# Two attention and token-MLP layers on one core: the order of SyncE's final waits

## The chip, the core and the metric

The kernel runs on one core of one Trainium2 chip. Five engines work side by side in that core, each through an instruction stream of its own: TensorE (PE), VectorE (DVE), ScalarE (ACT), GpSimd (POOL) and SyncE (SP). They are ordered among each other by semaphores alone. SyncE does no arithmetic here: it issues all the transfers (DMAs) and waits on semaphores. The metric is the device time of one execution in microseconds (us); lower is better.

## The reference, cut to what matters

```
x = A_x                                            # 1 x 2048 x 512, bf16
x = x + A(layernorm(x)); x = x + B(layernorm(x))   # layer 1
x = x + A(layernorm(x)); x = x + B(layernorm(x))   # layer 2, same weights
A: 32 heads of width 16, each query sees the 256 positions up to its own;
   softmax, times V, times wo (512 x 512)
B: h = layernorm(x); u = gelu(h^T . w1 (2048 x 1792) + b1); y = u . w2 (1792 x 2048) + b2; x + y^T
```

A mixes positions inside a window, B mixes all positions for each of the 512 columns. The result, 2048 x 512 in bf16, is 2 MB.

## The kernel before

The 2048 positions stand as 16 blocks of 128 on the partitions; x stays in on-chip memory (`x_sb`) through both layers and is written to the output (`out_dram`) only in the last stage. Attention goes through the sequence in chunks of 4 or 8 windows of 64 queries: scores on TensorE (L705), the exponential on ScalarE (L720), masks on GpSimd (L741), the product with V on TensorE (L758), then a transpose and a division. Between those, TensorE takes projection, wo and MLP matmuls (all of them through the helper at L526) as filler. The MLP's first product ends in L908, its gelu in L923. Its second product, y, is made a block of 128 positions at a time: fourteen matmuls add up into one bank of the accumulator, VectorE adds bias and residual (`resy`, L949) and SyncE stores the block (L997). The last block, `y_last`, is cut into pieces of 256, 128 and 128 columns, each with its own addition (L935) and its own store (L938). So the output leaves in 15 stores of 128 rows x 512 columns and 3 smaller ones.

Every operation is recorded in a `Graph`, and a list stored with the kernel (`ORDER`) fixes in which order each engine takes them. `Graph.emit` then writes the five streams. It gives every transfer one of 24 semaphores (`NDMA`), in turn: transfer number n, in SyncE's order, raises semaphore n modulo 24, and `rr` is the count of transfers at the end. A semaphore's transfer may only be issued when the one 24 before it has landed. `dcnt[k]` is the value that semaphore k has when all its transfers have landed.

When SyncE has issued its last transfer it waits, in the last lines of `emit`, until each of the 24 semaphores has its full count (L252). Then it leaves the block by a branch (L339) and meets the other four engines at a barrier, which ends the program. The barrier is run by GpSimd: it waits until all have signalled and then releases them.

The waits of those last lines are not written into the program in the order in which the loop names them. [...] In the program as built, that list is for the kernel before, from the first to the last:

```
12 | 13, 11 | 14, 10 | 15, 9 | 16, 8 | 17, 7 | 18, 6 | 19, 5 | 20, 4 | 21, 3 | 22, 2 | 23, 1 | branch: 0
```

That is: the names 0 to 23 of the loop come out from the middle of the list to its two ends. The last transfer of this kernel, the store of the last 128 columns, raises semaphore 13; the one before it, a store of a whole block, raises 12.

Of the kernel before, what the change touches and what calls it, by code (L numbers as in the profile page):

```python
# [93 lines left out]
class Graph:  # L94
# [104 lines left out]
    def emit(self, block):  # L199
        mark = {}  # L200
        cnt = {e: 0 for e in self.ENGS}
        dcnt = [0] * self.NDMA
        dlast = [None] * self.NDMA
        rr = 0
        for e in self.ENGS:
            for o in self.order[e]:
                if o.dma:
                    k = rr % self.NDMA
                    rr += 1
                    if dlast[k] is not None:  # L210
                        o.extra.append(dlast[k])
                    dlast[k] = o
                    dcnt[k] += 16 * o.parts
                    mark[o.idx] = (("d", k), dcnt[k])
                else:
                    cnt[e] += 1
                    mark[o.idx] = (e, cnt[e])

        know = {e: {} for e in self.ENGS}
        at_issue = {}  # L220
        waits = {}
        for o in sorted(self.ops, key=lambda o: o.pos):
            e = o.eng
            need = [d for d in {x.idx: x for x in o.deps + o.extra}.values() if not (e == "tensor" and d.eng == "tensor")]
            kn = know[e]
            best = {}
            for d in sorted(need, key=lambda d: -d.pos):
                s, v = mark[d.idx]
                if kn.get(s, 0) >= v:
                    continue  # L230
                best[s] = v
                kn[s] = v
                for s2, v2 in at_issue[d.idx].items():
                    if kn.get(s2, 0) < v2:
                        kn[s2] = v2
            waits[o.idx] = list(best.items())
            at_issue[o.idx] = dict(kn)
        sem = lambda s: self.dsem[s[1]] if isinstance(s, tuple) else self.sem[s]
        decs = {"sync": block.sync, "tensor": block.tensor, "vector": block.vector, "scalar": block.scalar,
                "gpsimd": block.gpsimd}  # L240
        for e in self.ENGS:
            def body(eng, e=e):
                for o in self.order[e]:
                    for s, v in waits[o.idx]:
                        eng.wait_ge(sem(s), v)
                    ins = o.fn(eng, o.cols32) if o.flex else o.fn(eng)
                    for i in ins if o.parts > 1 and o.dma else [ins]:
                        i.then_inc(sem(mark[o.idx][0]), 16 if o.dma else 1)
                if e == "sync":
                    for k in range(self.NDMA):  # L250
                        if dcnt[k]:
                            eng.wait_ge(self.dsem[k], dcnt[k])  # L252
            decs[e](body)
# [777 lines left out]
```

## Time and profile before

| what | us |
|---|---|
| median of 3 runs | 434.5 (434.42 to 434.79) |
| the profiled execution, its own time | 434.05 |
| its span, from the first instruction to the last | 432.3 |
| last TensorE matmul begins | 428.9 |
| last VectorE instruction ends | 429.5 |
| last store issued by SyncE, from and to | 429.64, 430.07 |
| last store landed | 431.19 |
| SyncE's branch out of the block | 431.90 |

The profile names an engine's instructions by the line of the kernel that made them. "L252 SPq" is SyncE's own queue at line 252: the semaphore-only instructions of the final waits. The start that a row gives for a waiting instruction is the moment at which its waits were over, as the rows of the end show: each begins right behind what it waited for. Semaphore and branch instructions aren't counted as busy time of an engine, so the page's first table, in which PE has 98% of the span, does not contain them; they are found by asking for their line, or by asking who waited for whom. The trace gives instructions and landings in nanoseconds, and the times with two or three decimals in this text are from it.

### The profile page before, as it was taken

The page shows a single profiled execution, that of the slowest core. Times are in us where ns is not written, and L with a number is a line of the kernel's source. Part 1 is how long each engine was busy: PE and PEld are TensorE (multiplying, and loading weights), DVE is VectorE, ACT ScalarE, POOL GpSimd, SP SyncE. Part 2 cuts the span into 40 slices and gives each one's busy share as a digit, 9 for nine tenths or more (in the row PEclk, how much of TensorE's full clock was granted, in tenths as well). Part 3 has the DMA queues.
Part 4 walks back from the last instruction along what each step waited for, and adds up shares of the span by engine and source line. Part 5 has one row for each costly group of instructions (what it writes and reads, how often), then busy time and mean ns, then how long its engine had stood idle before and what let it go on. Part 6 is the DMA issues. An engine that isn't in the chain of part 4 may idle for free.

```text
span 432.3 us, 14319 instructions
## 1 busy us (share of the span) xinstructions
PE 422.5 (98%) x6192; PEld 189.1 (44%) x6192; DVE 302.6 (70%) x566; ACT 324.0 (75%) x375; POOL 240.0 (56%) x359
## 2 busy tenths in 40 slices
PE   8898999999999999999999999999999999999997
PEld 7444444443434444443444444443443444444453
DVE  7999988997789868637565868788876377512133
ACT  4999999999998965509989999999999961330000
POOL 5698959697796651002677588778794741000000
PEclk9999999999999999999999999999999999999999
DMA  8735613540322556435352340330221455772453
GB/s 250 205 63 91 150 41 71 100 106 15 83 46 52 137 144 174 136 73 155 72 153 59 101 111 2 80 50 3 55 64 38 123 150 151 201 217 65 125 155 109
DMA packets 95023, 45.12 MB, mean 104 GB/s; under 512 B 27888, under 2 KB 94960, under 8 KB 94960
## 3 DMA queue, kind: packets, MB, share of 16 engines
q1 hardware_dynamic: 94960, 44.20, 39.9%
q8 instruction: 49, 0.80, 0.8%
q14 instruction: 14, 0.11, 0.1%
HBM read 33.56 MB, written 2.10 MB: 82 GB/s over the span
## 4 chain that ended last, share of the span: by engine, by line
PE 87%; ACT 8%; DVE 3%; POOL 1%; DMA 0%; issue 0%
PE PS L526 60%; PE PS L705 10%; PE PS L758 8%; PE PS L908 8%; ACT pt L720 7%; POOL pt L741 1%; DVE xh_sb L499 1%; DVE rl L796 1%; DMA x_sb<-in_A_x_dram 0%; DVE stats L475 0%; ACT kbd L596 0%; ACT vst L645 0%; DVE x_sb L949 0%; DVE vst L643 0%; DVE qT L586 0%
## 5 line engine op out<-in xcount | busy, mean ns | idle before, releaser
L720 ACT ACTIVATE pt<-PS 128x1024 bf16<-128x1024 f32 (+1 forms) x304 | 282.7, 1032 | 9.5 <-PE PS L705 7.6
L741 POOL TENSOR_TENSOR pt<-pt,ldm 128x256 int32<-128x256 int32 (+2 forms) x266 | 176.4, 690 | 55.7 <-ACT pt L720 52.1
L526 PE MATMUL PS<-xh_sb,w1b 128*128 128x512 bf16 x292 | 72.6, 381 | 0.1
L526 PE MATMUL PS<-uT,w2b 128*128 128x512 bf16 (+2 forms) x308 | 68.2, 360 | 0.0
L526 PE MATMUL PS<-xhT,wqkv 128*128 128x512 bf16 (+1 forms) x288 | 66.7, 357 | 0.8 <-DVE rl L796 0.4
L705 PE MATMUL PS<-qT,kbd 32*128 32x64 bf16 (+4 forms) x1552 | 60.2, 247 | 2.6 <-ACT pt L720 1.3
L949 DVE SCALAR_TENSOR_TENSOR x_sb<-PS,b2col,x_sb 128x512 bf16<-128x512 f32 x31 | 22.8, 748 | 55.6 <-PE PS L526 55.5
L492 POOL TENSOR_TENSOR rstd<-agg,mhalf 128x2 f32<-128x2 f32 (+1 forms) x34 | 23.4, 691 | 56.8 <-DVE agg L478 56.6
L705 PEld LDWEIGHTS PS<-qT,kbd 32*128 32x128 bf16 x1552 | 22.7, 92 | 61.1 <-ACT pt L720 44.0
L796 DVE STREAM_TRANSPOSE rl<-PS 128x1024 f32<-128x1024 f32 x31 | 38.5, 1242 | 14.0 <-PE PS L758 13.7
L758 PE MATMUL PS<-pt,vb 64*17 64x128 bf16 (+4 forms) x3104 | 44.0, 248 | 1.2 <-ACT pt L720 0.9
L526 PEld LDWEIGHTS PS<-uT,w2b 128*128 128x128 bf16 x308 | 27.6, 98 | 31.9 <-issue 3.2
L475 DVE BATCH_NORM_STATS2 stats<-x_sb 128x6 f32<-128x512 bf16 x62 | 40.9, 675 | 0.9 <-DMA x_sb<-in_A_x_dram 0.5
L526 PE MATMUL PS<-uT,pt 128*128 128x512 bf16 x168 | 40.8, 379 | 0.0
L758 PEld LDWEIGHTS PS<-pt,vb 64*17 64x17 bf16 x3104 | 31.6, 84 | 17.9 <-ACT pt L720 6.2
L526 PEld LDWEIGHTS PS<-xh_sb,w1b 128*128 128x128 bf16 x292 | 24.7, 97 | 32.8 <-issue 5.4
L526 PEld LDWEIGHTS PS<-xhT,wqkv 128*128 128x128 bf16 x288 | 24.3, 97 | 28.4 <-issue 5.3
L526 PE MATMUL PS<-wqkv,xhT 128*128 128x512 bf16 x128 | 34.4, 381 | 0.6 <-ACT pt L720 0.5
L908 PE MATMUL PS<-xh_sb,w1b 128*128 128x512 bf16 x156 | 34.6, 379 | 0.0
L923 ACT ACTIVATE uT<-rl,b1col 128x512 bf16<-128x512 f32 x28 | 18.1, 711 | 21.5 <-DVE rl L919 21.3
L526 PE MATMUL PS<-wo_sb,oT 128*128 128x512 bf16 x128 | 33.4, 381 | 0.0
L499 DVE TENSOR_SCALAR xh_sb<-x_sb,agg,rstd 128x512 bf16<-128x512 bf16 x64 | 28.8, 473 | 2.6 <-POOL rstd L492 2.5
(70 smaller groups left out, 331.6 us busy)
## 6 DMA issues: line engine op xcount, KB each, us to landing
w1b<-in_B_w_dram SPq DMA_DIRECT2D x109, 128.0 KB, 2.7
w2b<-in_B_w_dram SPq DMA_DIRECT2D x70, 128.0 KB, 2.7
pt<-in_B_w_dram SPq DMA_DIRECT2D x42, 128.0 KB, 3.2
vb<-vst SPq DMA_DIRECT2D x64, 68.0 KB, 2.1
out_dram<-x_sb SPq DMA_DIRECT2D x15, 128.0 KB, 1.9
x_sb<-in_A_x_dram SPq DMA_DIRECT2D x3, 512.0 KB, 6.7
wqkv<-in_A_wqkv_dram SPq DMA_DIRECT2D x4, 256.0 KB, 4.4
wqkv<-in_A_wqkv_dram SPq DMA_DIRECT2D x1, 512.0 KB, 5.8
```

Of the source, the lines that this page charges most:

```text
L475: op("vector:stat", lambda e: e.bn_stats(st[:, 0:6], bank(ft) if ft else x_sb[:, t, :]), reads=[ft or f"x{t}"], writes=[("st", i)], cost=d ...
L492: op("gpsimd:rstd", lambda e: e.tensor_tensor(rstd[:, t0:t1, 0], agg[:, t0:t1, 1], mhalf[:, 0:1].to_broadcast([P, t1 - t0]), op=ALU.pow), ...
L499: op("vector:xh", lambda e: e.tensor_scalar(xh_sb[:, t, :], x_sb[:, t, :], agg[:, t, 0:1], rstd[:, t, :], op0=ALU.subtract, op1=ALU.mult), ...
L526: return e.matmul(o, lhsT=w, rhs=x, start=start, stop=stop, skip_group_check=True)
L705: last = e.matmul(bank(tt[r // 2], r % 2)[:, base + c0 * 64:base + (c0 + n) * 64], lhsT=kbd[32 * r:32 * r + 32, tk[0][o].slot, jj].rearran ...
L720: op("scalar:exp", lambda e, ts=ts, tp=tp, i=i, cols=cols: e.activation(probs(tp)[:, i, 0:cols, :], pair(ts)[:, :, 0:cols].rearrange("p r ...
L741: return e.tensor_tensor(v, v, m, op=ALU.mult)
L758: last = e.matmul(bank(t, h)[32 * r:32 * r + 17, i + q0 * 64:i + (q0 + n) * 64], lhsT=vb[64 * h:64 * h + 64, tk[1].slot, jj, 4 * o + r, :] ...
L796: op("vector:od", lambda e, t=tod, tr=tr: e.transpose(rl[:, tr.slot:tr.slot + 2].rearrange("p a b -> p (a b)"), pair(t)), reads=[(tod, i) ...
L908: last = e.matmul(bank(tu, tt), lhsT=v()[:, sc - b0, k0 + tt * P:k0 + (tt + 1) * P], rhs=xh_sb[:, sc, :], start=(sc == b0), stop=(sc == NT ...
L923: op("scalar:gelu", lambda e, ft=ft, tt=tt: e.activation(uT[:, ft, :], rl[:, tmps[tt].slot], ACTF.Gelu_apprx_tanh, bias=b1col[:, ft:ft + 1 ...
L949: op("vector:resy", lambda e: e.scalar_tensor_tensor(x_sb[:, t, :], bank(ft), b2col[:, t:t + 1], x_sb[:, t, :], op0=ALU.add, op1=ALU.add), ...
```

## The change

The loop over the 24 semaphores at the end of `emit` no longer names them from 0 to 23, but in a list that starts from the last transfer:

```
--- before.py
+++ after.py
@@ -247,7 +247,8 @@
                     for i in ins if o.parts > 1 and o.dma else [ins]:
                         i.then_inc(sem(mark[o.idx][0]), 16 if o.dma else 1)
                 if e == "sync":
-                    for k in range(self.NDMA):
+                    late = [(rr - 1 - j) % self.NDMA for j in range(self.NDMA)]
+                    for k in late[:1] + late[1::2] + late[2::2][::-1]:
                         if dcnt[k]:
                             eng.wait_ge(self.dsem[k], dcnt[k])
             decs[e](body)
```

`late` is 13, 12, 11, ... down to 0, then 23, ... down to 14: the semaphores from the last transfer's backwards. The loop names 13 first, then 12, 10, 8 and so on, and the odd places from the far end last. After the same spreading from the middle to the two ends, the list in the program as built is

```
14 | 15, 16 | 17, 18 | 19, 20 | 21, 22 | 23, 0 | 1, 2 | 3, 4 | 5, 6 | 7, 8 | 9, 10 | 11, 12 | branch: 13
```

It is the order in which the last 24 transfers were issued. There are twelve semaphore-only instructions and a branch as before, and the streams of the five engines are otherwise the same, row by row. All lines behind the edit have a number that is higher by one (L997 becomes L998).

More of the change, by code (lines that the diff above doesn't have):

```diff
@@ L249, in body @@
                 if e == "sync":
-                    for k in range(self.NDMA):
+                    late = [(rr - 1 - j) % self.NDMA for j in range(self.NDMA)]
+                    for k in late[:1] + late[1::2] + late[2::2][::-1]:
                         if dcnt[k]:
```

## The prediction

> **What bounds the kernel now.** I read the page's totals and the chain first, to see what the span is made of; then the last 12 us of SyncE's queue in order of time, who waited for whom there, and last the final waits and the branch by their lines.
>
> ```profile
> span 432.3 us, 14319 instructions
> PE 422.5 (98%) x6192; PEld 189.1 (44%) x6192; DVE 302.6 (70%) x566; ACT 324.0 (75%) x375; POOL 240.0 (56%) x359
> PE 87%; ACT 8%; DVE 3%; POOL 1%; DMA 0%; issue 0%
> ```
>
> TensorE bounds 98% of the span. The edit touches none of its instructions, so nothing can be won there; all that the change can move lies behind the last matmul (begun at 428.9). That stretch of 3.4 us, in order of time on VectorE and then on SyncE:
>
> ```profile
> 428.48 0.75 DVE L949 SCALAR_TENSOR_TENSOR x_sb<-PS,b2col,x_sb 128x512 bf16<-128x512 f32 x1 [2.01 <-PE PS L526]
> 429.15 0.35 DVE L935 SCALAR_TENSOR_TENSOR x_sb<-PS,b2col,x_sb 128x128 bf16<-128x128 f32 x1
> ```
>
> ```profile
> 429.64 0.43 SPq L938 DMA_DIRECT2D out_dram<-x_sb  x1
> ```
>
> ```profile
> SPq L252 <- DMA out_dram<-x_sb: 1.1, 2, 0.9
> SPq L339 <- PEq L339: 0.2, 1, 0.2
> ```
>
> VectorE is done at 429.50. SyncE is free of its last store's issue at 430.07 and then waits for transfers just twice: 0.9 us for semaphore 12 (landed 430.97) and 0.2 us for semaphore 13 (landed 431.19, 1.56 us after that store's issue began). Nothing moves any data after 431.19, but the span goes on for 1.1 us. What fills it, by the lines of the final waits (first the whole group, then the stretch from 431.25 to 431.85 alone) and of the block's end:
>
> ```profile
> L252 SPq EVENT_SEMAPHORE  x12: 17/28/28, 431.0 to 431.8; - x12
> ```
>
> ```profile
> L252 SPq EVENT_SEMAPHORE  x10: 28/28/28, 431.3 to 431.8; - x10
> ```
>
> ```profile
> L339 SPq COMPARE_BRANCH  x1: 41/41/41, 431.9 to 431.9; - x1
> L339 SPq DRAIN  x1: 7/7/7, 432.1 to 432.1; - x1
> L339 POOLq EVENT_SEMAPHORE  x2: 17/17/17, 432.1 to 432.2; - x2
> ```
>
> The reader is to see that ten of the twelve wait instructions come after the last landing. Every semaphore they name had been full for long: the latest of them is semaphore 10, at 427.94. They are not waiting, they are being executed, one behind the other, on the path that ends the program. The barrier is not held by another engine: GpSimd's instruction that gathers the signals begins at 432.11, 32 ns after SyncE's drain at 432.08, and VectorE, the last of the others, had drained at 429.6.
>
> **The change, part by part.** The starts of that tail are 430.981 (wait for 12), 431.207 (13 and 11, 16 ns after 13 landed), then 431.280, 431.344, 431.406, 431.465, 431.526, 431.586, 431.647, 431.706, 431.768, 431.827, and the branch at 431.895. From one start to the next it is 59 to 73 ns, of which 28 are busy.
>
> *What leaves the path.* Behind the landing of 13 stand today the pair that names 13, ten more pairs, and the branch. In the built order after the change only the branch stands there, and it carries the wait for 13. It can begin when the pair with 13 begins today: 431.207, against 431.895. That is eleven steps, 73 + 64 + 62 + 59 + 61 + 60 + 61 + 59 + 62 + 59 + 68 = 688 ns. So the first term is -0.69 us.
>
> *What takes their place beside the store.* The first eleven wait instructions (14 to 10) now run from 430.07. All their semaphores are full by then (the latest at 427.94), so they need eleven steps of about 61 ns, 0.67 us, and are done near 430.75. The twelfth (11 and 12) waits until 12 lands: 430.97, begins at 430.98. One step of 61 to 73 ns later, by 431.05, SyncE stands at the branch, 0.14 us before 13 lands. So the cover is 430.07 to 430.97, 0.90 us for 0.67 us of steps; if it were gone (a landing right after the issue) up to all 0.69 us would come back. I cost this part at nothing.
>
> *Does SyncE at work delay the last store?* [...] Issue to landing of the whole-block stores tells: followed at once by another issue they took 1.81 to 1.85 us (the five from 422.6 to 424.1) and 1.71 (429.26); followed by an idle queue, 1.83 (424.59) and 1.81 (426.87). Of the 128-column stores, the one with an issue behind it took 1.44 and the one without 1.56. A busy queue costs them nothing that shows; the bounds are -0.12 and +0.12 us, and I take 0.
>
> *The branch that now waits.* Its 181 ns until the drain, and the barrier behind it, stay. The trace of before has no branch that waits; the nearest rows are the pair that waited for 13 (begun 16 ns after the landing) and the drain (181 ns after the branch began). Between 0 and 0.18 us could be lost if a waiting branch had to start its work anew, and as much won if part of the 181 ns ran during the wait. I take 0, by the pair, which waited on the very same semaphore.
>
> *The price of a step without the profiler.* Each instruction leaves a record in the profile, and the plain runs have no trace. From below, eleven instructions cost their busy time, 11 x 28 = 0.31 us; from above they cost the steps, 0.69 us, with the branch's 0.18 at most 0.87. I take the steps.
>
> Sum against the profiled execution: 434.05 - 0.69 = 433.36 us, its span 432.30 - 0.69 = 431.61, with the same 1.75 us around it. That execution lies 0.45 us under the median of the three runs, so the forecast on their scale is 434.5 - 0.69 = 433.8 us, 0.16% faster.
>
> **The rivals.** *Nothing comes of it (434.5).* Two ways lead there. The source names semaphore 13 first, not last; if that order were kept, all twelve other waits would follow the landing, 61 ns more than today. The built order, which for the loop 0 to 23 gives 12 first and 0 last, just as the profile's rows have it, says otherwise. Or the 1.75 us around the span ends on something that does not begin at the barrier's end; no row shows that stretch.
>
> *Each semaphore is read by itself, at a price that is not hidden (about 432.8).* Ten pairs, the 11 beside 13, and the branch's 0 make 22 names behind the landing, and 21 of them leave, since 13's own check and the branch remain. The longest step of a single unblocked wait in the trace is 82 ns (the one at 0.70 us, before a DMA's issue): 21 x 82 = 1.72 us. Against it: a pair costs 59 to 73 ns in all and 11 ns of busy time more than a single wait (28 against 17), so by the rows a name is no unit of cost. [...]
>
> *The last store lands later (435.4 and above).* [...] To make the kernel slower at all the landing must slip by 0.69 us, to be slower by over 0.2% by 1.56, which would double its 1.56. The twelve hundredths between stores with and without a busy queue speak against it.
>
> **How the numbers follow.** A measurement of this kernel can tell about 0.2% (0.87 us) from no change. The forecast case, a gain between 0.31 and 0.87, gets 0.80; nothing comes of it 0.10; more than the trace shows (a dearer read, a branch that gains) 0.05; a later store 0.05. The forecast lies only 0.18 us on the near side of the bound, and the three runs shown span 0.37, with the profiled execution 0.37 under the lowest; so of the 0.80 about 0.36 would be read as faster by over 0.2%. Together: faster 0.36 + 0.05 = 0.41, same 0.44 + 0.10 = 0.54, and slower 0.05. The range holds the gains from 0 (434.5) to 0.87 with half a microsecond of scatter beyond it (433.1).
>
> **What would show it.** In the changed profile, eleven of the twelve waits of that line start between 430.1 and 430.8 on the old scale, the twelfth follows semaphore 12, and the branch starts within 20 ns of the last landing; the drain follows it by 0.18, and span minus last landing falls from 1.11 to 0.42 us. The wait of the branch's line for the last store appears as 0.1 to 0.2 us. TensorE's rows must not move. The prediction is wrong if the last store takes clearly more than 1.56 us, if the branch-to-drain step grows, or if the span shrinks and the time does not.

## The result, and the profile after

| | before | after |
|---|---|---|
| median of 21 runs each, us | 434.5 (434.1 to 435.65) | 434.06 (433.36 to 434.62) |
| ratio to before | | 0.9985, 95% interval 0.9979 to 0.9992 |
| the profiled execution: span, us | 432.30 | 432.50 |
| VectorE's last result | 429.50 | 430.40 |
| last landing | 431.19 | 432.09 |
| SyncE's branch | 431.90 | 432.10 |
| last landing to the end of the span | 1.106 | 0.413 |

The kernel is 0.15% faster. The interval goes from 0.08 to 0.21%: zero is outside it, so there is a gain, and nearly all of it lies under the 0.2% named as the bound. The ratio stands for 0.65 us, next to the forecast 0.69; it comes from all the runs, and the two medians alone differ by less, 0.44 us. The spans of the two profiled executions say the opposite at first sight: the changed one is 0.2 us longer. It came to its last VectorE result 0.90 us later, for a reason ahead of the change's place (last section), and gave 0.69 back in the last microsecond. So the reading has to start from the last landing, not from the span.

The changed kernel's end, in order of time on VectorE and SyncE:

```profile
429.38 0.75 DVE L950 SCALAR_TENSOR_TENSOR x_sb<-PS,b2col,x_sb 128x512 bf16<-128x512 f32 x1 [2.01 <-PE PS L527]
430.05 0.35 DVE L936 SCALAR_TENSOR_TENSOR x_sb<-PS,b2col,x_sb 128x128 bf16<-128x128 f32 x1
430.16 0.33 SPq L998 DMA_DIRECT2D out_dram<-x_sb  x1
430.54 0.43 SPq L939 DMA_DIRECT2D out_dram<-x_sb  x1
```

Its final waits, now at L253 (in both traces a row of them names one semaphore or two, and the branch names one): first all twelve, then those in the stretch from 430.9 to 431.66 alone:

```profile
L253 SPq EVENT_SEMAPHORE  x12: 17/28/193, 431.0 to 431.7; - x12
```

```profile
L253 SPq EVENT_SEMAPHORE  x11: 17/28/28, 431.0 to 431.6; - x11
```

The block's end (now L340) on SyncE, and SyncE's waits (us in total, times, longest; `PEq L340` is the barrier, whose release is GpSimd's instruction at 432.39, though the view names TensorE's queue for it):

```profile
L340 SPq COMPARE_BRANCH  x1: 41/41/41, 432.1 to 432.1; - x1
L340 SPq DRAIN  x1: 7/7/7, 432.3 to 432.3; - x1
```

```profile
SPq L253 <- DMA out_dram<-x_sb: 0.2, 1, 0.2
SPq L340 <- DMA out_dram<-x_sb: 0.2, 1, 0.2
SPq L340 <- PEq L340: 0.2, 1, 0.2
```

Before, eleven instructions of the group began after the last landing: the pair that had waited for it, 16 ns later, and the ten in the second of the two lines shown for L252. The branch found its semaphore full. Now all twelve begin between 431.02 and 431.70, ahead of the landing at 432.09, and it is the branch that waits for the last store. It begins at 432.101, 16 ns after the landing.

### The profile page after: what moved, and what is told of

The parts are those of the page before. It is cut to its first block, busy times and chain, and to the rows that moved or that the text cites. A ratio compares the mean times of both kernels' runs of the same rounds, so it can differ in the third digit from the quotient of the medians.

```text
span 432.5 us, 14247 instructions
## 1 busy us (share of the span) xinstructions
PE 413.7 (96%) x6120; PEld 188.5 (44%) x6192; DVE 302.8 (70%) x566; ACT 324.3 (75%) x375; POOL 240.2 (56%) x359
## 4 chain that ended last, share of the span: by engine, by line
PE 83%; ACT 8%; DVE 4%; issue 2%; POOL 1%; DMA 1%; SPq 0%
PE PS L527 58%; PE PS L706 10%; PE PS L759 8%; PE PS L909 8%; ACT pt L721 7%; POOL pt L742 1%; DVE xh_sb L500 1%; DMA x_sb<-in_A_x_dram 1%; DVE rl L797 1%; ACT kbd L597 0%; DVE x_sb L950 0%; DVE stats L476 0%; DVE uT L898 0%; DVE oT L808 0%; ACT vst L646 0%
## 5 line engine op out<-in xcount | busy, mean ns | idle before, releaser
L527 PE MATMUL PS<-xh_sb,w1b 128*128 128x512 bf16 x273 | 68.9, 380 | 2.9 <-issue 2.3
L527 PE MATMUL PS<-uT,w2b 128*128 128x512 bf16 (+2 forms) x298 | 66.8, 359 | 1.0 <-issue 0.6
L527 PE MATMUL PS<-xhT,wqkv 128*128 128x512 bf16 (+1 forms) x272 | 64.2, 355 | 3.2 <-issue 1.7
L909 PE MATMUL PS<-xh_sb,w1b 128*128 128x512 bf16 x154 | 34.7, 379 | 0.1
L527 PE MATMUL PS<-wqkv,xhT 128*128 128x512 bf16 x118 | 32.7, 381 | 1.9 <-ACT pt L721 1.1
L527 PE MATMUL PS<-wo_sb,oT 128*128 128x512 bf16 x118 | 31.5, 380 | 1.6 <-issue 0.8
```

The lines of the kernel that those rows point to most:

```text
L527: return e.matmul(o, lhsT=w, rhs=x, start=start, stop=stop, skip_group_check=True)
L909: last = e.matmul(bank(tu, tt), lhsT=v()[:, sc - b0, k0 + tt * P:k0 + (tt + 1) * P], rhs=xh_sb[:, sc, :], start=(sc == b0), stop=(sc == NT ...
```

## The experiments

Two theories stood against each other. By the first, "steps" in the texts below, each wait instruction behind the last landing costs about 61 ns of the kernel's end, whatever it waits for. By the second the order is nothing, and the 0.15% belongs to what differs in the body from one execution to the next. Three smaller questions were open: whether the measured times pay the whole step or only its 28 busy ns, a price per semaphore name, and whether SyncE at work gets in the way of the store it has just issued.

All experiments but the last edit only which waits `emit` gives and where. A helper `spread(built)` names them so that the program as built has them in the order `built`; `old` is the 24 semaphores in the order of their last transfers, 14 to 23, then 0 to 13. In the excerpts of code a minus marks a line of the changed kernel, and the helper's own lines are left out. Times behind the landing are the profiled execution's, ratios are to the kernel before on the same chip.

### The last store's wait first

```
-                    for k in late[:1] + late[1::2] + late[2::2][::-1]:
+                    for k in spread(old[-1:] + old[:-1]):      # built: 13 | 14, 15 | ... | 10, 11 | branch: 12
```

> Built order of the final waits: 13 (the last store) alone in the first instruction, then 14 to 11 in pairs, 12 on the branch. Steps (each wait instruction behind the last landing costs about 61 ns of the end, profiled or not): twelve steps follow the landing, 12 x 61 = 0.73 us, one more than before; from the last landing to the end of the span 0.016 + 0.73 + 0.40 = 1.15 us (before 1.11, after 0.41); the time is that of before, ratio 1.000 (+0.05 us). Order is nothing (the 0.15% came from what differs in the body between executions): the ratio to before is about that of the changed kernel, 0.9985. Name by name: as steps, since all names stand behind the landing.

Measured: 434.64 us, ratio 1.0002 (0.9993 to 1.0011); 1.159 us from the landing to the end (1.15 expected). The group of this line (L260 here), in which the first instruction alone waits and the other eleven follow in an unbroken row:

```profile
L260 SPq EVENT_SEMAPHORE  x12: 17/28/28, 431.8 to 432.5; - x12
```

```profile
SPq L260 <- DMA out_dram<-x_sb: 1.1, 1, 1.1
```

The edit has the same waits as the changed kernel and only another order, and the whole gain is gone. That speaks for steps.

### Five more rounds of waits behind the landing

```
+                    for k in spread([12, 13, 11, 14, 10, ..., 23, 1, 0] + old * 5):   # the order of before, then 60 more pairs
```

> The 24 waits in the order of before, and then all 24 five times more, in the order of the transfers: 60 more instructions of two waits each, all behind the last landing, all long satisfied. Steps: 60 x 61 ns = 3.66 us more; 4.77 us from the last landing to the end of the span; the plain runs 3.7 us slower than before, ratio 1.0084. Busy time alone in plain runs (the rest of a step is the profiler's): the profile as above, but the plain runs 60 x 28 ns = 1.7 us slower, 1.0039. Order is nothing, the end is set elsewhere: 1.000. [...]

Measured: 438.43 us, ratio 1.0087 (1.0073 to 1.0101); 4.726 us from the landing to the end (4.77 expected).

```profile
L260 SPq EVENT_SEMAPHORE  x72: 17/28/28, 431.3 to 435.8; - x72
```

```profile
SPq L260 <- DMA out_dram<-x_sb: 1.1, 2, 0.9
```

In the profile, the 71 steps from the pair with 13 (431.566) to the branch (435.878) take 60.7 ns each. In the measured times 60 more instructions cost 438.43 - 434.65 = 3.78 us, 63 ns each (53 to 73 by the interval); in the median span they cost 436.45 - 432.9 = 3.55 us, 59 ns each. So the device time pays the whole step, and not the 28 ns of busy time, which would have given 1.0039.

What a step costs with the profiler off is not shown: each of these executions, of this kernel and of the one before, has a measured span and a granted clock, as the profiled one has, so none of them is known to have run without the profiler's records.

A read for each name at the 82 ns of the prediction's rival is out too: 120 names would have cost 9.84 us, ratio 1.0226; they took 3.78 us, 32 ns each. That it is the instruction that is paid, and not the name, is seen in the changed kernel's profile: there the first wait names one semaphore and the next instruction begins 59 ns later, and behind the pairs the next begins 59 to 72 ns later. "Order is nothing" is out a second time.

### Most waits moved ahead of the last two stores

```
                     for s, v in waits[o.idx]:
                         eng.wait_ge(sem(s), v)
+                    if e == "sync" and o is self.order[e][-2]:
+                        for k in [(rr + j) % self.NDMA for j in range(self.NDMA - 4)]:   # 14 to 9
+                            eng.wait_ge(self.dsem[k], dcnt[k])
...
+                    for k in (13, 12, 10, 11):      # built: 10 | 11, 12 | branch: 13
```

> The twenty waits for semaphores 14 to 9 are moved ahead of the last whole-block store, where SyncE stands idle for VectorE; behind the last store stay 10, then 11 and 12, then 13 on the branch. SyncE so has next to nothing to do while the last store is on its way. Steps: the same end as in the changed kernel, 0.42 us from the last landing to the end of the span, ratio to before 0.998 to 0.999. Waits in the store's way (executing eleven waits right behind the last issue delays that store): here the last store, from the start of its issue to its landing, is faster than the 1.55 us of the changed kernel's profile by what the waits cost it, and the time is below the changed kernel's. Order is nothing: 1.000 or any value unlike the changed kernel's.

Measured: 433.94 us, ratio 0.9983 (0.9974 to 0.9992); 0.417 us behind the landing. Its waits at the very end (L255), and SyncE's queue:

```profile
L255 SPq EVENT_SEMAPHORE  x2: 17/420/824, 430.9 to 431.0; - x2
```

```profile
430.44 0.42 SPq L941 DMA_DIRECT2D out_dram<-x_sb  x1
```

The last store took 1.552 us from the start of its issue to its landing with SyncE all but idle, against 1.549 in the changed kernel with SyncE executing eleven waits. In the other profiles it is the same: 1.549 to 1.555 us where SyncE stood still, or nearly so, behind the last issue, 1.549 to 1.558 where it executed waits. Nothing shows that the waits get in the store's way.

### The changed kernel again

> The changed kernel once more, on the same chip as the others of this call. Steps: 0.41 us from the last landing to the end of the span, ratio 0.9984. Order is nothing: 1.000 as likely as 0.997, with e1_last_first on the same side.

Measured: 433.95 us, ratio 0.9987 (0.9978 to 0.9996), 0.414 us behind the landing. A third set of runs, on another chip beside the version with ScalarE's store:

> The changed kernel beside the version with ScalarE's store. Steps: ratio to before 0.9984, from the last landing to the end of the span 0.41 us, from VectorE's end 2.10 us.

Measured: 433.88 us, ratio 0.9987 (0.9978 to 0.9996), 0.418 us behind the landing, 2.11 us from VectorE's end to the end of the span. Three sets and the version above lie at 0.9983 to 0.9987; the two orders with the last store's wait early lie at 1. The ratio 0.9984 that the profile's 0.69 us makes is inside each interval.

### Half of the waits behind the last store

```
+                    for k in spread(old[:11] + old[-2:] + old[11:-2]):   # built: ... 23, 0 | 12, 13 | 1, 2 | ... | 9, 10 | branch: 11
```

> The waits for 12 and 13, the last two stores, share one instruction in the middle of the list; behind it stand five pairs (1 to 10) and the branch with 11, all long satisfied; ahead of it six instructions. Steps: six steps behind the landing, 0.016 + 6 x 61 ns + 0.40 = 0.79 us from the last landing to the end of the span, between 1.11 (before) and 0.41 (changed). A cost that hangs on whether the branch itself waits (and not on the number of steps): 1.11, as before, since here too the branch finds its semaphore full.

Measured: 0.761 us behind the landing (0.79 expected). The one execution took 434.81 us, which is inside the scatter of the kernel before on that chip (434.04 to 435.32); a single time tells nothing here. The stretch from 432.05 to 432.2 shows the pair with 12 and 13 alone:

```profile
L260 SPq EVENT_SEMAPHORE  x1: 222/222/222, 432.1 to 432.1; - x1
```

This pair begins when 12 is full and waits for 13 inside its 222 ns, and so the sixth step is not all behind the landing: five pairs begin after it. The end falls in between, as the count of steps has it, although the branch here waits for no transfer. A cost that hangs on the branch's own wait is excluded.

### More waits than the store can cover

```
+                    for k in spread(old[:22] * 2 + old[:2] + old[-2:]):   # built: 24 instructions ..., 11, 14 | 15, 12 | branch: 13
```

> The changed order with 22 long satisfied names repeated ahead of the last two: 24 wait instructions in place of 12 between the last store's issue and the branch, which still carries 13. Steps with a cover of about 1.1 us: the first begins 0.05 us behind the issue, the twenty-fourth 23 x 61 ns = 1.40 us later, which is 1.89 us from the start of the issue, when the store has landed for 0.34; five or six of them and the branch follow the landing; 0.80 us from the last landing to the end of the span. Waits in the store's way: the store takes longer than 1.55 us from issue to landing, by as much as SyncE is kept busier. If all waits ahead of the branch were free: 0.41 us.

Measured: 0.797 us behind the landing (0.80 expected); store 1.555 us from issue to landing. The one execution took 434.03 us; VectorE's last result came at 429.82 in it and at 430.63 in the one of the section above, so these two times can't be compared. The stretch from 431.52 on, behind the landing at 431.51:

```profile
L260 SPq EVENT_SEMAPHORE  x6: 28/28/28, 431.5 to 431.8; - x6
```

SyncE's waits at these lines name no transfer any more; only the barrier is left:

```profile
SPq L347 <- PEq L347: 0.2, 1, 0.2
```

The last wait stands last here too, but six steps and the branch spill over the cover. So it isn't the order in itself that pays: the changed kernel's twelve wait instructions all fit beside the store (0.413 us behind the landing), and of the 24 here six did not (0.797).

### The last store from ScalarE

What is left is the store's 1.55 us, 0.42 us of branch and barrier, and 0.13 us between VectorE's last result and the last issue, because SyncE is still issuing the store before (until 430.49 in the changed kernel's profile, where the result came at 430.40 and the last issue begins at 430.54). The last was tried: ScalarE issues the store of the last 128 columns and waits for it, and SyncE ends on 12.

```
-                for o in self.order[e]:
+                tail = self.order["sync"][-1]
+                for o in self.order[e][:-1] if e == "sync" else self.order[e] + [tail] if e == "scalar" else self.order[e]:
...
-                    late = [(rr - 1 - j) % self.NDMA for j in range(self.NDMA)]
+                    late = [(rr - 2 - j) % self.NDMA for j in range(self.NDMA - 1)]
...
+                if e == "scalar":
+                    k = (rr - 1) % self.NDMA
+                    eng.wait_ge(self.dsem[k], dcnt[k])
```

> The last store, of the last 128 columns, is issued by ScalarE, idle since 382 us, and ScalarE waits for it; SyncE ends on the wait for 12. What is left of the end is then tried: in the changed kernel that store's issue starts 0.13 us after VectorE's last result, because SyncE is still issuing the store before it. Steps: ScalarE starts within 0.03 us of the result, the store lands 1.55 us later as before, and from VectorE's end to the end of the span it is 2.0 us in place of 2.1; the time 0.1 us below the changed kernel's, which the rounds can't tell from it. If a first transfer from another queue is dearer, or if both stores' packets get into each other's way, the landing is later and the end 2.1 us or more.

Measured: 433.85 us, ratio 0.9988 (0.9979 to 0.9997), beside 0.9987 for the changed kernel in the same group. The end in order of time, and the block's end on both engines:

```profile
429.23 0.35 DVE L940 SCALAR_TENSOR_TENSOR x_sb<-PS,b2col,x_sb 128x128 bf16<-128x128 f32 x1
429.33 0.33 SPq L1002 DMA_DIRECT2D out_dram<-x_sb  x1
429.61 0.37 ACTq L943 DMA_DIRECT2D out_dram<-x_sb  x1
```

```profile
L344 SPq COMPARE_BRANCH  x1: 41/41/41, 431.1 to 431.1; - x1
L344 ACTq COMPARE_BRANCH  x1: 33/33/33, 431.2 to 431.2; - x1
```

ScalarE issues 0.03 us after the result, 0.10 earlier than SyncE did. But the store takes 1.62 us in place of 1.55, and the other one, issued 0.27 us ahead of it, 1.73 in place of 1.71. From VectorE's end to the end of the span it is 2.06 us against 2.10. Of the 0.10 us, 0.07 went into the store's longer time to its landing; the 0.03 to 0.05 us that remain at the end of the span can't be measured in the time. That the two stores get into each other's way, or that another queue's first store is dearer, was not told apart.

## Why the prediction was right

*What leaves the path* is shown, in size too: eleven steps were to go, 0.688 us, and the time behind the landing fell from 1.106 to 0.413 us, which is 0.693. The order reversed takes it back (1.159), half of it takes back half (0.761).

*The price of a step without the profiler* was the widest bound, 0.31 to 0.87. In the measured times the whole step is paid: 63 ns by the dose, 61 in its profile, and 0.65 us by the ratio. But the term took the runs of the median for runs without the profiler's records, and no run here is known to be one. So the choice of the steps is borne out for the time as it was measured; whether a step is cheaper with the profiler off stays open.

*The cover* held: eleven waits from 431.02 to 431.66, where about 430.07 to 430.75 was forecast on a scale 0.90 us earlier. Its edge lies where the steps say, as the 24 instructions showed. One detail was read wrongly. The twelfth instruction (11, 12) was to begin at the landing of 12; it began at once, at 431.697, 60 ns behind the row before, when 11 had been full since 429.57, and lasted 193 ns, to 22 ns after 12 had landed at 431.868. This row began with its first name full and held the wait for the second, as the 222 ns of the pair with 12 and 13 did in the half order. So the sentence ahead of the prediction, that a row's start is the moment at which its waits were over, is too wide: it fits the pair of before only because 13 is named first there and 11 was long full. The sum does not hang on it, since the last wait stands alone on the branch.

*SyncE at work does not delay the store*: 1.549 to 1.558 us in the profiles with the waits beside it, 1.552 with SyncE idle. The bounds of 0.12 on either side were far too wide. The rows on which they rest are four stores from 422.6 to 424.1, not five, with 1.81 to 1.85 us; a fifth, at 421.79, also followed at once by another issue, took 1.73. That doesn't move the term.

*The branch that waits* cost nothing of its own: 16 ns from landing to branch, 177 ns from there to the drain (181 before).

The forecast time, 433.8, stands 0.26 us under the 434.06 that came out. Medians of the two kernels in the three groups differ by 0.44 (434.5 - 434.06), 0.70 (434.65 - 433.95) and 0.64 us (434.52 - 433.88), so a quarter of a microsecond is what such a difference of medians moves by from group to group, as the range had allowed; the step behind the landing does not. The sum against the profiled execution (a span of 431.61) meets the same scatter: the three profiled spans of the changed kernel are 432.50, 431.52 and 432.49. One sign named in advance fails by its letter for that reason: TensorE's rows were not to move, and its last matmul begins 0.90 us later in the first of these profiles and 0.09 earlier in the second, with the whole body ahead of it. Of the rivals, the read for each name was excluded by the dose, the later store by the landings, and "nothing comes of it" by all intervals. Between faster and same by 0.2% the forecast had left the case open, with 0.54 for same: 0.13 to 0.15% is under the bound in all three sets, and the intervals reach from 0.04% to 0.22%.

## What to carry to other kernels

A wait on a semaphore that had long been full still cost its instruction here, 59 to 73 ns from one start to the next in the profile of before and 63 ns of device time in the dose, and at the end of this program each one stood behind the last landing when the list as built named the last transfer early: eleven steps, 0.69 us. Name the transfers in the order in which they land and the last store's wait last, and look at the built order, for here the loop's order was not the one that was executed: of 0 to 23, SyncE's rows have 12 first and 0 last. Such a gain of a tenth of a per cent is read from the last landing to the end of the span, which repeated here to 0.005 us, and not from the span, which moved by more than the gain.

## What had not been expected

The body scatters by more than the change is worth. The same changed kernel had profiled spans of 431.52 and 432.50 us. VectorE's statistics at the start wait for the first loads of x, and these waits differ; before, after and the second run of the changed kernel:

```profile
DVE stats L475 <- DMA x_sb<-in_A_x_dram: 0.5, 1, 0.5
```

```profile
DVE stats L476 <- DMA x_sb<-in_A_x_dram: 1.1, 3, 0.6
```

```profile
DVE stats L476 <- DMA x_sb<-in_A_x_dram: 0.5, 1, 0.5
```

From before to after, VectorE's same instruction (the second block's statistics, at 3.7 us) is 0.45 us later. The shift then moves between 0.41 and 0.72, stands at 0.60 at 16.4 us and at 0.72 at 377.9, and is 0.90 from 379.9 to the end: the last 0.18 us comes in one wait of VectorE, for TensorE's MLP product (1.30 us in the profile of before, 1.48 in that of after). From the second run to the first of the changed kernel it is 0.47 at the same place, 0.73 at 16.4 and 0.99 at the end. So some two thirds of the shift are there within the first 17 us, and all of it ahead of the last stage; none of it is where the edit is. Why the loads land at different times, and why TensorE comes later at 379.9, was not tried.
